# Dilated sliding attention into a two-layer feed-forward: new loads, transposes, masks and order for the first batches, and joined attention bursts

## Chip, core and metric

One core of one Trainium2 chip. The time is device microseconds (us) of the whole program. Before the change it is 368.92 us, the median of 3 runs (368.79 to 369.2).

## What is computed

```python
# q, k, v: (8 batches, 8 heads, 576 positions, 64), float32
scores = q @ k.T / sqrt(64)
rel = pos[:, None] - pos[None, :]
mask_plain = (rel >= 0) & (rel < 32)                      # heads 0-3
mask_dil = (rel >= 0) & (rel < 128) & (rel % 4 == 0)      # heads 4-7
attn = softmax(where(mask, scores, -1e9)) @ v
x = attn.transpose(0, 2, 1, 3).reshape(4608, 512)
h = x @ w_in                                               # (512, 2048)
out = maximum(0.01 * h, h) @ w_out                         # (2048, 512)
```

## The kernel before

Everything is float16 on TensorE (PE) with float32 sums. The attention is cut into 64 units. A number `n` = 2 * batch + kind names half a batch: four heads with the plain mask (kind 0) or with the dilated one (kind 1). A unit `u` is one pair of heads (`p`) and one half of the positions (288 of 576) of an `n`; there are 4 units in an `n` and 8 in a batch.

For each `n`, `load` fetches q, k and v on SP's queue, `cast_qk` and `cast_v` make them float16, and q and k are transposed so that the 64 head dimensions lie on partitions: for `n` < 4 (`NPE`) by PE (`pe_transpose`: six 96x96 blocks for two heads, then one copy from PSUM that spreads each block over every sixth column), later by a DMA transpose. `scores(u)` makes the 288 score columns of two heads in `sps` (six matmuls of 96 columns, or eight of 72 for kind 1), ACT takes the exponential (`er`), DVE multiplies by a 0/1 mask (`em`). `values(u)` makes the weighted values `o` and the sums `den`, takes the reciprocal (by ln and exp on ACT for batch 0, by DVE's reciprocal later) and DVE writes the product into `xT`. `sps`, `o` and `den` have one buffer each.

The feed-forward works on 9 chunks of 512 tokens. A chunk is 32 pieces of four matmuls with 512 columns: 16 of `ff_in` (one of 16 blocks of hidden units; ACT applies the leaky ReLU into `gt`), then 16 of `ff_out` (four groups of 128 tokens, each in four parts; ACT copies the sum to `ob`, and SP stores it). Chunk 0 needs all units of batch 0; chunk 1 needs batch 1 as well.

The order is written out by hand; each engine runs its instructions in this order, and SP issues its DMAs in it. Before the loop come the loads of batch 0, of w_in and w_out (1 MiB pieces through two staging buffers `wf`, so a third piece waits for the cast of the first) and of batch 1 (`load(2)`, `load(3)`), and the 8 units of batch 0. In the loop over chunks, chunk 0 has the work on batch 1 put between its pieces, two pieces to a unit of its second half; from chunk 1 on there are four pieces to a unit:

```python
if i % per == 0:
    if u + 1 < NU:
        scores(u + 1)
    prefetch(u // 4, u % 4)
if i % per == per // 2:
    values(u, False)
    u += 1
f()
```

So `scores` of the next unit and `values` of this one stand two pieces (8 matmuls) apart. After unit 63, in chunk 7, only feed-forward pieces are left.

Of the kernel before, what the change touches and what calls it, by code (L numbers as in the profile page):

```python
# [14 lines left out]
WIN = 32  # L15
# [6 lines left out]
CH = 512  # L22


@with_exitstack
def kernel(ctx: ExitStack, tc: tile.TileContext, q, k, v, w_in, w_out, out):
# [10 lines left out]
    ctx.enter_context(tc.manual_schedule())  # L37

    nc.scalar.preload_act_table_set("natural_log_exp_and_others")
    ones = cst.tile([128, 64], FP16, name="ones")  # L40
    nc.gpsimd.memset(ones, 1.0)

    mask = cst.tile([128, 3, 96], FP16, name="mask")
    nc.gpsimd.memset(mask, 1.0)
    nc.gpsimd.affine_select(out=mask, in_=mask, pattern=[[0, 3], [1, 96]], base=32,
                            channel_multiplier=-1, compare_op=ALU.is_ge, fill=0.0)
    nc.gpsimd.affine_select(out=mask, in_=mask, pattern=[[0, 3], [-1, 96]], base=-1,
                            channel_multiplier=1, compare_op=ALU.is_ge, fill=0.0)
    nc.gpsimd.memset(mask[0:32, 0, :], 0.0)
    ident = cst.tile([96, 96], FP16, name="ident")  # L50
    nc.gpsimd.memset(ident, 0.0)
    nc.gpsimd.affine_select(out=ident, in_=ident, pattern=[[-1, 96]], base=0,
                            channel_multiplier=1, compare_op=ALU.not_equal, fill=1.0)
# [3 lines left out]
    NPE = 4  # L57
# [12 lines left out]
    def load(n):  # L70
        b, kind = divmod(n, 2)
        base = (b * H + 4 * kind) * S * D
        for nm, x in (("q", q), ("k", k)):
            t = stg.tile([96, 24, D], FP32, tag=nm + "f")
            if n < NPE:
                nc.sync.dma_start(t.rearrange("p (h t) d -> p h (t d)", h=4),  # L76
                                  rows_ap(x, base, [[6 * D, 96], [S * D, 4], [1, 6 * D]]))
            else:
                nc.sync.dma_start(t, rows_ap(x, base, [[D, 96], [96 * D, 24], [1, D]]))
            qkf[n, nm] = t  # L80
        t = stg.tile([128, 32, D], FP32, tag="vf")
        vf[n] = t
        if kind == 0:
            s = base - 32 * D
            if s >= 0:
                nc.sync.dma_start(t[:, 0:24, :], rows_ap(v, s, [[D, 128], [96 * D, 24], [1, D]]))
            else:
                nc.gpsimd.memset(t[0:32, 0, :], 0.0)
                nc.sync.dma_start(t[32:128, 0, :], rows_ap(v, 0, [[D, 96], [1, D]]))
                nc.sync.dma_start(t[:, 1:24, :],  # L90
                                  rows_ap(v, s + 96 * D, [[D, 128], [96 * D, 23], [1, D]]))
        else:
            t4 = t.rearrange("p (g r) d -> p g (r d)", r=4)
            s = base - 128 * D
            if n < 2 * B - 1:
                nc.sync.dma_start(t4, rows_ap(v, s, [[4 * D, 128], [288 * D, 8], [1, 4 * D]]))
            else:
                nc.gpsimd.memset(t[96:128, 28:32, :], 0.0)
                nc.sync.dma_start(t4[:, 0:7, :],
                                  rows_ap(v, s, [[4 * D, 128], [288 * D, 7], [1, 4 * D]]))  # L100
# [4 lines left out]
    def cast_qk(n, *engs):  # L105
        for nm, eng in zip(("q", "k"), engs):
            t = att.tile([96, 2, 6, 2, D], FP16, tag=nm + "h", bufs=1)
            f = qkf.pop((n, nm))
            for p in range(2):
                src = f[:, 12 * p:12 * p + 12, :].rearrange("p (h t) d -> p h t d", h=2)  # L110
                dst = t[:, p].rearrange("p t h d -> p h t d")
                eng(out=dst, in_=src)  # L112
            qkh[n, nm] = t

    def cast_v(n, eng):
        t = att.tile([128, 32, D], FP16, tag="vh", bufs=3)
        m = 32 if n % 2 else 24
        eng(out=t[:, 0:m, :], in_=vf.pop(n)[:, 0:m, :])  # L118
        vh[n] = t

    def transpose(n):
        for nm, dst in (("q", qT), ("k", kT)):
            o = dst[n % NB][:, PAD:PAD + 2 * S].rearrange("p (c r) -> p c r", r=96)
            nc.sync.dma_start_transpose(
                o, qkh.pop((n, nm)).rearrange("p a t h d -> p (a t h d)"))

    def pe_transpose(n, p, nm, eng):

        h = qkh[n, nm]
        o = (qT if nm == "q" else kT)[n % NB][:, PAD + S * p:PAD + S * p + S]  # L130
        tp = psm.tile([128, 1024], FP16, tag="pm", name="tp")
# [7 lines left out]
    ems = {}  # L139

    def scores(u):
        n, p, half = u // 4, (u // 2) % 2, u % 2
        kind = n % 2
        sps = psa.tile([128, 2, 512], FP32, tag="sps")
        tok = PAD + S * p + HALF * half
        for j in range(4 if kind else 3):
            w = 72 if kind else 96
            for hh in range(2):
# [7 lines left out]
                nc.tensor.matmul(sps[:, hh, w * j:w * j + w], ka, qa, start=True, stop=True)  # L156
        er = att.tile([128, 2, HALF], FP16, tag="er", bufs=3)
        nc.scalar.activation(out=er, in_=sps[:, :, 0:HALF], func=AF.Exp, scale=SCALE)  # L158
        em = att.tile([128, 2, HALF], FP16, tag="em", bufs=3)
# [13 lines left out]
    def values(u, log_recip):  # L173
# [4 lines left out]
        o = psa.tile([128, 512], FP32, tag="o")  # L178
        den = psa.tile([128, 512], FP32, tag="den")
# [6 lines left out]
        for hh in range(2):  # L186
            nc.tensor.matmul(den[64 * hh:64 * hh + 64, 0:HALF], ones, em[:, hh, :],  # L187
                             start=True, stop=True)
        rec = att.tile([128, HALF], FP32, tag="rec")
        if log_recip:  # L190
            ln = att.tile([128, HALF], FP32, tag="ln")
# [17 lines left out]
    def load_w(i, g):  # L209
        t = stg.tile([128, 4, 512], FP32, tag="wf", bufs=2)  # L210
        if i == 0:
            src = rows_ap(w_in, 512 * g, [[DFF, 128], [128 * DFF, 4], [1, 512]])
        else:
            src = rows_ap(w_out, 512 * g * DM, [[DM, 128], [128 * DM, 4], [1, DM]])
        nc.sync.dma_start(t, src)
        wst[i, g] = t

    def cast_w(i, g, eng):
        eng(out=(w1, w2)[i][g], in_=wst.pop((i, g)))  # L219

# [3 lines left out]
    def ff_in(c, j):  # L224
# [3 lines left out]
        for i in range(4):  # L228
            nc.tensor.matmul(hp, w1[j // 4][:, i, 128 * (j % 4):128 * (j % 4) + 128],  # L229
# [5 lines left out]
    def ff_out(c, t, part):  # L235
# [6 lines left out]
        if part == 3:  # L242
            ob = moe.tile([128, DM], FP32, tag="ob", bufs=3, name="ob")
# [12 lines left out]
    V, P, A = nc.vector.tensor_copy, nc.gpsimd.tensor_copy, nc.scalar.copy  # L256
    load(0)
    load(1)
    for g in range(4):
        load_w(0, g)  # L260
    cast_qk(0, V, A)
    cast_v(0, P)
    for p in range(2):
        pe_transpose(0, p, "q", V)
        pe_transpose(0, p, "k", A)
    cast_qk(1, P, P)
    cast_v(1, P)
    scores(0)
    scores(1)
    for u in range(8):  # L270
        if u == 2:
            for p in range(2):
                pe_transpose(1, p, "k", A)
                pe_transpose(1, p, "q", V)
        if u + 2 < 8:
            scores(u + 2)
        values(u, True)
        if u == 3:
            cast_w(0, 0, P)
# [90 lines left out]
```

## Time and profile before

| | |
|---|---|
| median of 3 runs | 368.92 us |
| profiled execution: time / span | 367.16 / 365.5 us |
| PE busy / DVE / ACT / POOL | 320.9 / 213.5 / 160.0 / 86.1 us |
| feed-forward matmuls (L229, L240) | 1152 of 128x512, 385 ns each as recorded |
| units of attention | 64, of which 8 before chunk 0 |
| bytes read from HBM / written | 41.91 / 9.44 MB |

The span runs from the first instruction to the last; the rest of the profiled execution's time, 1.66 us, lies around it. Matmuls overlap in the pipeline, so their cost is read from the distance of their starts, not from the recorded duration. The profile's name `t` is that of any staging or float16 tile of q, k, v and the weights.

### The profile page before, as it was taken

How to read it: one execution, taken by the hardware profiler on the slowest of the kernel's cores; microseconds unless marked ns; L12 is line 12 of the kernel's file. 1: busy time of each engine (PE TensorE's matmuls, PEld its weight loads, DVE VectorE, ACT ScalarE, POOL GpSimd, SP SyncE). 2: the span in 40 equal slices, each digit the busy share in tenths (PEclk: the TensorE clock that was granted, in tenths of full speed). 3: DMA queues.
4: the chain of work that ended last, by engine and by line, in shares of the span. 5: the costliest groups of instructions: out<-in, count | busy, mean ns of one | idle time of the engine just before them, and what ended most of it. 6: DMA issues, size and time to landing. Idle time of an engine off the chain costs nothing.

```text
span 365.5 us, 5534 instructions
## 1 busy us (share of the span) xinstructions
PE 320.9 (88%) x2272; PEld 141.3 (39%) x2272; DVE 213.5 (58%) x204; ACT 160.0 (44%) x267; POOL 86.1 (24%) x97
## 2 busy tenths in 40 slices
PE   0453938857799999999999999999999999999995
PEld 0342314423344444444444444444444444444442
DVE  2575319999867777677667768766776674000000
ACT  1884623103365247425632562276236523713621
POOL 3442225545325031505220523045000000000000
PEclk9999987889999999999999999999999999999999
DMA  8984899999999289939972998495140011011011
GB/s 192 269 318 153 296 286 247 294 227 277 239 236 241 73 163 217 223 105 231 259 187 79 211 218 199 118 224 119 43 138 0 2 59 58 0 51 66 0 42 76
DMA packets 129727, 58.79 MB, mean 161 GB/s; under 512 B 109757, under 2 KB 120997, under 8 KB 129701
## 3 DMA queue, kind: packets, MB, share of 16 engines
q1 hardware_dynamic: 129701, 58.43, 63.9%
q8 instruction: 18, 0.29, 0.3%
q14 instruction: 8, 0.07, 0.1%
HBM read 41.91 MB, written 9.44 MB: 141 GB/s over the span
## 4 chain that ended last, share of the span: by engine, by line
PE 72%; DVE 11%; DMA 5%; ACT 5%; SPq 3%; issue 2%; POOL 0%; POOLq 0%; ACTq 0%
PE hp L229 31%; PE op L240 31%; DVE rec L195 5%; PE o L184 4%; PE sps L156 4%; DMA t<-in_k_dram 4%; SPq L76 3%; DVE xT L199 2%; PE den L187 2%; ACT kT L135 2%; DMA t<-in_moe_w_out_dram 1%; DVE qT L135 1%; ACT rec L193 1%; ACT ln L192 1%; DVE xT L202 1%
## 5 line engine op out<-in xcount | busy, mean ns | idle before, releaser
L229 PE MATMUL hp<-xT,w 128*128 128x512 f16 x576 | 137.0, 385 | 1.5 <-DVE xT L199 1.3
L240 PE MATMUL op<-w,gt 128*128 128x512 f16 x576 | 137.9, 385 | 0.0
L195 DVE RECIPROCAL rec<-den 128x288 f32<-128x288 f32 x56 | 109.5, 1955 | 42.0 <-PE den L187 42.0
L231 ACT ACTIVATE gt<-hp 128x512 f16<-128x512 f32 x144 | 86.0, 597 | 58.5 <-PE hp L229 57.7
L112 POOL CAST t<-t 96x768 f16<-96x768 f32 x58 | 48.8, 876 | 137.8 <-DMA qT<-t 122.7
L229 PEld LDWEIGHTS <-w 128*128 128x128 f16 x576 | 52.6, 99 | 65.1 <-issue 5.3
L240 PEld LDWEIGHTS <-gt 128*128 128x128 f16 x576 | 51.6, 98 | 62.2 <-issue 2.3
L244 ACT COPY ob<-op 128x512 f32<-128x512 f32 x36 | 21.1, 585 | 110.9 <-PE op L240 95.0
L158 ACT ACTIVATE er<-sps 128x576 f16<-128x576 f32 x64 | 42.0, 656 | 18.3 <-PE sps L156 18.3
L165 DVE TENSOR_TENSOR em<-er,mask 128x576 f16<-128x576 f16 x48 | 27.1, 564 | 13.7 <-ACT er L158 13.3
L184 PE MATMUL o<-em,t 128*64 128x72 f16 (+1 forms) x448 | 21.6, 216 | 14.7 <-DVE xT L199 7.8
L156 PE MATMUL sps<-qT,kT 64*128 64x72 f16 (+1 forms) x448 | 24.4, 231 | 6.3 <-ACT er L158 3.4
L118 POOL CAST t<-t 128x1536 f16<-128x1536 f32 (+1 forms) x16 | 27.0, 1688 | 9.2 <-DMA t<-in_v_dram 9.2
L184 PEld LDWEIGHTS <-t 128*64 128x64 f16 x448 | 13.9, 115 | 39.3 <-issue 13.3
L199 DVE TENSOR_TENSOR xT<-o,rec 128x288 f16<-128x288 f32 x32 | 25.7, 802 | 5.8 <-ACT rec L193 4.8
L156 PEld LDWEIGHTS <-kT 64*128 64x128 f16 x448 | 13.7, 109 | 31.1 <-issue 27.4
L133 PE MATMUL tp<-ident,t 96*128 96x96 f16 x96 | 8.5, 256 | 18.1 <-DVE t L112 14.2
L187 PE MATMUL den<-em,ones 128*64 128x288 f16 x128 | 20.3, 308 | 0.0
L135 DVE COPY qT<-tp 128x576 f16<-128x576 f16 x8 | 16.6, 2116 | 1.8 <-PE tp L133 1.8
L202 DVE TENSOR_TENSOR xT<-o,rec 128x288 f16<-128x288 f32 x32 | 14.6, 458 | 3.7 <-ACT rec L193 2.6
L133 PEld LDWEIGHTS <-t 96*128 96x128 f16 x96 | 7.0, 126 | 22.0 <-DVE t L112 14.6
L219 POOL CAST w<-t 128x2048 f16<-128x2048 f32 x4 | 7.6, 1893 | 21.7 <-DMA t<-in_moe_w_out_dram 15.9
(25 smaller groups left out, 54.0 us busy)
## 6 DMA issues: line engine op xcount, KB each, us to landing
t<-in_q_dram SPq DMA_DIRECT2D x16, 576.0 KB, 5.3
t<-in_k_dram SPq DMA_DIRECT2D x16, 576.0 KB, 7.1
out_dram<-ob SPq DMA_DIRECT2D x36, 256.0 KB, 2.0
t<-in_v_dram SPq DMA_DIRECT2D x7, 1024.0 KB, 9.0
t<-in_v_dram SPq DMA_DIRECT2D x7, 768.0 KB, 7.4
t<-in_moe_w_in_dram SPq DMA_DIRECT2D x4, 1024.0 KB, 11.3
t<-in_moe_w_out_dram SPq DMA_DIRECT2D x4, 1024.0 KB, 7.0
t<-in_v_dram SPq DMA_DIRECT2D x1, 896.0 KB, 8.3
```

Source lines behind the costliest of these rows:

```text
L112: eng(out=dst, in_=src)
L135: eng(out=o.rearrange("p (r t) -> p t r", t=6), in_=tp[:, 0:S].rearrange("p (t r) -> p t r", t=6))
L156: nc.tensor.matmul(sps[:, hh, w * j:w * j + w], ka, qa, start=True, stop=True)
L158: nc.scalar.activation(out=er, in_=sps[:, :, 0:HALF], func=AF.Exp, scale=SCALE)
L165: nc.vector.tensor_tensor(out=em.rearrange("p h (t c) -> p (h t) c", c=w), in0=er.rearrange("p h (t c) -> p (h t) c", c=w), in1=mb, op=ALU ...
L184: nc.tensor.matmul(o[64 * hh:64 * hh + 64, w * j:w * j + w], vt[:, sl, :], em[:, hh, w * j:w * j + w], start=True, stop=True)
L187: nc.tensor.matmul(den[64 * hh:64 * hh + 64, 0:HALF], ones, em[:, hh, :], start=True, stop=True)
L195: nc.vector.reciprocal(out=rec, in_=den[:, 0:HALF])
L199: nc.vector.tensor_tensor(out=x, in0=o[:, 0:HALF].rearrange("p (r u) -> p r u", r=4), in1=rec.rearrange("p (r u) -> p r u", r=4), op=ALU.mult)
L229: nc.tensor.matmul(hp, w1[j // 4][:, i, 128 * (j % 4):128 * (j % 4) + 128], xT[:, i, CH * c:CH * c + CH], start=(i == 0), stop=(i == 3))
L231: nc.scalar.activation(out=gts[c][:, j, :], in_=hp, func=AF.Prelu, alpha=0.01)
L240: nc.tensor.matmul(op, gts[c][:, j, 128 * t:128 * t + 128], w2[j // 4][:, j % 4, :], start=(j == 0), stop=(j == 15))
```

## The change

- For `n` < 5 q and k are loaded with nine rows (2304 B) to each of 128 partitions, where it was six rows (1536 B) on 96; batch 0 comes in four parts, one pair of heads each, q, k, v together. The PE transposes become 18 of 64x64 for a pair, and the copy from PSUM reads every 64th element and writes contiguously.
- Batch 0: a matmul of the identity with a bias tile (0 or -30000) opens each `sps`, the scores add to it, and the multiplication by the mask on DVE is gone. `o` and `den` come from the pool of four PSUM buffers. Reciprocals of units 1 and 4 are on DVE. More constants are built on POOL.
- 16 matmuls on a tile of zeros open the program.
- `wf` has three buffers; batch 1 is queued ahead of w_out; w_out is read in runs of 8 KiB to a partition. w_in's columns are taken with step 4 to fit.
- Chunk 0 is written out: 16 `ff_in`, units 8 and 9 bare, then `ff_out` in the order of the parts of w_out with four sums open, a unit to every two pieces. Batch 2's first half is transposed by PE in chunk 1, which has three pieces to a unit.
- From then on, `scores(u + 1)`, `values(u)` and the mask of `u + 1` (`masked`) follow on each other, four pieces apart; `den` comes before `o`. `ob` has two buffers instead of three.

```diff
-    NPE = 4
+    NPE = 5
...
+            elif len(pairs) == 2:
+                nc.sync.dma_start(t[:, 0:18, :].rearrange("p (a t) d -> p a (t d)", a=2),
+                                  rows_ap(x, base, [[9 * D, 128], [2 * S * D, 2], [1, 9 * D]]))
...
-        for t in range(6):
-            nc.tensor.transpose(tp[:, 96 * t:96 * t + 96],
-                                h[:, p, t].rearrange("p h d -> p (h d)"), ident)
-        eng(out=o.rearrange("p (r t) -> p t r", t=6),
-            in_=tp[:, 0:S].rearrange("p (t r) -> p t r", t=6))
+        for t in range(9):
+            for hh in range(2):
+                r = slice(64 * hh, 64 * hh + 64)
+                nc.tensor.transpose(tp[r, 64 * t:64 * t + 64], h[r, t, :], ident[r, r])
+        eng(out=o.rearrange("p (r t) -> p r t", t=9),
+            in_=tp[:, 0:S].rearrange("p (t r) -> p r t", t=9))
...
+        if pe_mask:
+            mb = ((bias0, bias), (bias40, bias4))[kind][half].rearrange("p a c -> p (a c)")
+            for hh in range(2):
+                nc.tensor.matmul(sps[:, hh, 0:HALF], ident, mb, start=True, stop=False)
...
-        t = stg.tile([128, 4, 512], FP32, tag="wf", bufs=2)
+        t = stg.tile([128, 4, 512], FP32, tag="wf", bufs=WF, name="wf")
...
-            nc.tensor.matmul(hp, w1[j // 4][:, i, 128 * (j % 4):128 * (j % 4) + 128],
+            nc.tensor.matmul(hp, w1[j // 4][:, i, j % 4::4],
...
+    castA(0)
+    transB(0)
+    castA(1)
+    C(0)
+    C(1)
+    transB(1)
+    Dv(0)
+    castA(2)
+    C(2)
+    Dv(1)
...
+    cast_w(0, 1, P)
+    load_qk(2)
+    load_v(2)
+    load_qk(3)
+    load_v(3)
+    cast_w(0, 2, V)
+    cast_w(0, 3, P)
+    for g in range(4):
+        load_w(1, g)
...
+    for g in range(4):
+        for t in range(4):
+            if t % 2 == 0 and u < 16:
+                if u + 1 < 16:
+                    scores(u + 1)
+                values(u, True)
+                if u + 1 < 16:
+                    masked(u + 1)
+                u += 1
...
+    for c in range(1, 9):
+        per, first = (3, 4) if c == 1 else (4, 0)
...
+            if u < NU and i >= first and (i - first) % per == 0 and not (c == 1 and i == 4):
+                if u + 1 < NU:
+                    scores(u + 1)
+                values(u, c == 1 and u % 2 == 0)
+                if u + 1 < NU:
+                    masked(u + 1)
+                prefetch(u // 4, u % 4)
+                u += 1
```

In the changed program `castA(x)` casts a pair of heads, `transB(x)` transposes it, `C(u)` is `scores` with the bias matmul and `Dv(u)` is `values` from the larger pool.

The order on SP's queue around the weights, before (L215 is `load_w`, the 96x4x384 loads are q and k of batch 1):

```order
L215 DMA t<-in_moe_w_in_dram 128x4x512 x4
L215 DMA t<-in_moe_w_out_dram 128x4x512 x4
L76 DMA t<-in_q_dram 96x4x384
L76 DMA t<-in_k_dram 96x4x384
L86 DMA t<-in_v_dram 128x24x64
```

The same place after:

```order
L255 DMA wf<-in_moe_w_in_dram 128x4x512 x4
L94 DMA qf<-in_q_dram 128x2x576
L94 DMA kf<-in_k_dram 128x2x576
L115 DMA vf<-in_v_dram 128x24x64
L94 DMA qf<-in_q_dram 128x2x576
L94 DMA kf<-in_k_dram 128x2x576
L126 DMA vf<-in_v_dram 128x8x256
L257 DMA wf<-in_moe_w_out_dram 128x2048 x4
```

Batch 1 moved from behind the four pieces of w_out to ahead of them.

PE in the loop around a burst of scores, before (`hp` and `op` are the sums of `ff_in` and `ff_out`):

```order
L229 MATMUL hp<-xT,w_0_101 128x512
L156 LDWEIGHTS kT_92
L156 MATMUL sps<-qT_89,kT_92 128x96
...
L229 LDWEIGHTS w_1_102
L229 MATMUL hp<-xT,w_1_102 128x512
```

and after:

```order
L189 LDWEIGHTS kT_117
L189 MATMUL sps<-qT_114,kT_117 128x96
L224 LDWEIGHTS ones
L224 MATMUL den<-em,ones 64x288
...
L230 LDWEIGHTS vh
L230 MATMUL o<-em,vh 64x72
L285 LDWEIGHTS gt
L285 MATMUL op<-w_0_129,gt 128x512
```

The scores are now followed by the sums and values of the unit before, and only then by feed-forward matmuls.

DVE in batch 0, before (L170 and L165 are the mask, L202 is xT, L135 the copy from PSUM):

```order
L112 CAST t<-t 96x2x6x64 x2
L135 COPY qT_89<-tp 128x6x96 x2
L170 TENSOR_TENSOR em<-er,mask 128x576
L165 TENSOR_TENSOR em<-er,mask 128x576
L170 TENSOR_TENSOR em<-er,mask 128x576
L202 TENSOR_TENSOR xT<-o,rec 128x288
```

and after:

```order
L136 CAST qh<-qf 128x576
L164 COPY qT_113<-tp 128x576
L136 CAST qh<-qf 128x576
L164 COPY qT_113<-tp 128x576
L164 COPY kT_116<-tp 128x576
L245 TENSOR_TENSOR xT<-o,rec 128x288
L136 CAST qh<-qf 128x576
L238 RECIPROCAL rec<-den 128x288
```

The masks are gone from DVE; casts of single pairs, more of the copies and two reciprocals stand there instead.

## Rows read from the trace of the kernel before

**Rows 1.** The page, part 2: 40 equal slices of the span (9.14 us each).

```profile
PE   0453938857799999999999999999999999999995
GB/s 192 269 318 153 296 286 247 294 227 277 239 236 241 73 163 217 223 105 231 259 187 79 211 218 199 118 224 119 43 138 0 2 59 58 0 51 66 0 42 76
```

**Rows 2.** Busy time of engines by stage; behind them granted clock, DMA share, GB/s.

```profile
0.00:38.20 38.20, 14.43 (x180) 9.83 (x181) 20.01 (x24) 21.85 (x31) 13.80 (x26) 1.00 0.80 240
38.20:96.70 58.50, 42.79 (x313) 18.53 (x312) 43.34 (x37) 16.77 (x29) 22.44 (x20) 0.88 1.06 264
96.70:361.50 264.80, 263.67 (x1786) 112.91 (x1780) 150.13 (x145) 120.75 (x207) 49.88 (x51) 1.00 0.54 128
361.50:365.50 4.00, 0.00 (x0) 0.00 (x0) 0.00 (x0) 0.58 (x1) 0.00 (x0) 1.00 0.17 68
```

**Rows 3.** Timeline of chunk 0's first half, engine by engine (start, duration, instruction).

```profile
32.21 13.86 SPq L215 DMA_DIRECT2D t<-in_moe_w_out_dram  x4
46.11 0.50 SPq L76 DMA_DIRECT2D t<-in_q_dram  x1
...
55.00 1.02 DVE L112 CAST t<-t 96x768 f16<-96x768 f32 x2 [1.08 <-DMA t<-in_q_dram]
...
55.61 0.66 PE L133 MATMUL tp<-ident,t 96*128 96x96 f16 x6 [7.14 <-DVE t L112]
...
66.99 1.89 POOL L118 CAST t<-t 128x2048 f16<-128x2048 f32 x1 [0.57 <-DMA t<-in_v_dram]
```

**Rows 4.** Groups of instructions by form: count, busy us, mean ns, idle before.

```profile
L195 DVE RECIPROCAL rec<-den 128x288 f32<-128x288 f32 x56 | 109.5, 1955 | 42.0 <-PE den L187 42.0
L158 ACT ACTIVATE er<-sps 128x576 f16<-128x576 f32 x64 | 42.0, 656 | 18.3 <-PE sps L156 18.3
L199 DVE TENSOR_TENSOR xT<-o,rec 128x288 f16<-128x288 f32 x32 | 25.7, 802 | 5.8 <-ACT rec L193 4.8
L135 DVE COPY qT<-tp 128x576 f16<-128x576 f16 x8 | 16.6, 2116 | 1.8 <-PE tp L133 1.8
L202 DVE TENSOR_TENSOR xT<-o,rec 128x288 f16<-128x288 f32 x32 | 14.6, 458 | 3.7 <-ACT rec L193 2.6
L135 ACT COPY kT<-tp 128x576 f16<-128x576 f16 x4 | 8.0, 2189 | 0.0
L112 DVE CAST t<-t 96x768 f16<-96x768 f32 x4 | 2.0, 552 | 7.5 <-DMA t<-in_q_dram 7.5
L112 ACT CAST t<-t 96x768 f16<-96x768 f32 x2 | 1.6, 828 | 6.9 <-DMA t<-in_k_dram 6.9
```

**Rows 5.** Timeline of ACT, end of batch 0.

```profile
33.93 0.41 ACT L192 ACTIVATE ln<-den 128x288 f32<-128x288 f32 x1 [1.61 <-PE den L187]
34.38 0.44 ACT L193 ACTIVATE rec<-ln 128x288 f32<-128x288 f32 x1
36.43 0.41 ACT L192 ACTIVATE ln<-den 128x288 f32<-128x288 f32 x1 [1.61 <-PE den L187]
```

**Rows 6.** Timeline of PE in the loop: eight matmuls and the scores after them.

```profile
134.97 1.90 PE L229 MATMUL hp<-xT,w 128*128 128x512 f16 x8
136.81 0.30 PE L156 MATMUL sps<-qT,kT 64*128 64x96 f16 x6
```

**Rows 7.** Timeline of ACT, end of chunk 8: two copies, 16 matmuls apart.

```profile
358.07 0.58 ACT L244 COPY ob<-op 128x512 f32<-128x512 f32 x1 [2.87 <-PE op L240]
361.52 0.58 ACT L244 COPY ob<-op 128x512 f32<-128x512 f32 x1 [2.87 <-PE op L240]
```

**Rows 8.** Timeline of PE: six transposes and what follows.

```profile
59.76 0.42 PE L133 MATMUL tp<-ident,t 96*128 96x96 f16 x6
60.01 1.03 PE L229 MATMUL hp<-xT,w 128*128 128x512 f16 x4
```

**Rows 9.** Timeline of DVE in chunk 0 (first), and the mask's line from 110 to 300 us.

```profile
87.36 1.70 DVE L165 TENSOR_TENSOR em<-er,mask 128x576 f16<-128x576 f16 x1
...
L165 DVE TENSOR_TENSOR em<-er,mask x34: 457/459/1731, 111.7 to 299.0; 128x576 f16<-128x576 f16 x34
```

More of the change, by code (lines that the diff above doesn't have):

```diff
@@ L177, in values @@
         vt = vh[n]
[L178 to L179 removed]
+        if pool is None:
+            o = psa.tile([128, 512], FP32, tag="o", name="o")
+            den = psa.tile([128, 512], FP32, tag="den", name="den")
+        else:
+            den = pool.tile([128, 512], FP32, tag="pm", name="den")
+            o = pool.tile([128, 512], FP32, tag="pm", name="o")
+        for hh in range(2):
+            nc.tensor.matmul(den[64 * hh:64 * hh + 64, 0:HALF], ones, em[:, hh, :],
+                             start=True, stop=True)
         for j in range(4 if kind else 3):
@@ L185, in values @@
                                  em[:, hh, w * j:w * j + w], start=True, stop=True)
[L186 to L189, printed above, removed]
+        rec = att.tile([128, HALF], FP32, tag="rec", name="rec")
         if log_recip:
-            ln = att.tile([128, HALF], FP32, tag="ln")
+            ln = att.tile([128, HALF], FP32, tag="ln", name="ln")
             nc.scalar.activation(out=ln, in_=den[:, 0:HALF], func=AF.Ln)
@@ new lines, with castA, transB, C @@
+    wp = psm.tile([128, 512], FP32, tag="pm", name="wp")
+    for _ in range(16):
+        nc.tensor.matmul(wp[0:64, 0:288], ones, warm, start=True, stop=True)
+    def castA(x):
+        n, p = divmod(x, 2)
+        cast_qk(n, "q", V, (p,))
+        cast_qk(n, "k", A, (p,))
+        cast_v(n, P, (p,))
+    def transB(x):
+        n, p = divmod(x, 2)
+        pe_transpose(n, p, "q", V)
+        pe_transpose(n, p, "k", V if x % 2 else A)
+    def C(u):
+        scores(u, True)
+    def Dv(u):
+        values(u, u not in (1, 4), psm)
@@ new lines @@
+    masked(8)
+    pe_transpose(3, 0, "q", V)
+    pe_transpose(3, 0, "k", A)
+    scores(9)
+    values(8, True)
+    masked(9)
+    pe_transpose(3, 1, "q", V)
+    pe_transpose(3, 1, "k", A)
+    scores(10)
+    values(9, True)
+    cast_v(3, P)
+    masked(10)
+    cast_w(1, 0, P)
+    load_qk(4)
+    load_v(4)
+    load_qk(5)
+    load_v(5)
+    u = 10
+    acc = [psm.tile([128, 512], FP32, tag="pm", name="op") for _ in range(4)]
+    for t in range(4):
+        ops[0, t] = acc[t]
+    for g in range(4):
+        for t in range(4):
+            if t % 2 == 0 and u < 16:
[5 more added lines that the diff above has]
+                u += 1
+            if t == 2 and g < 3:
+                cast_w(1, g + 1, P)
+            op = acc[t]
+            for j in range(4 * g, 4 * g + 4):
+                nc.tensor.matmul(op, gts[0][:, j, 128 * t:128 * t + 128], w2[g][:, j % 4, :],
+                                 start=(j == 0), stop=(j == 15))
+            if g == 3:
+                ob = moe.tile([128, DM], FP32, tag="ob", bufs=2, name="ob")
+                nc.scalar.copy(out=ob, in_=op)
+                nc.sync.dma_start(out[128 * t:128 * t + 128, :], ob)
```

292 lines of the change are left out of this document (154 added, 138 removed).

## The prediction

> **What bounds the kernel now.** I read the slices of the page first. PE's digits are 9 from about a quarter of the span to its end; before that they lie between 0 and 9 [rows 1]. The view by stages puts numbers to it: from 96.7 to 361.5 us PE is busy 263.67 of 264.8, in the 38.2 us of batch 0 only 14.43, and in chunk 0 (38.2 to 96.7) 42.79 of 58.5, at a mean granted clock of 0.88 against 1.00 afterwards; the last 4.0 us are a copy and a store [rows 2]. So the program is a start of 96.7 us in which PE waits, then a stretch in which PE is the bound.
>
> The start has two parts. In batch 0 nothing is saturated: DVE 20.01 and ACT 21.85 of 38.2 us [rows 2]. Its last units come every 2.5 us (ln at 33.93, the next at 36.43), and ACT waits 1.61 of these for the sums [rows 5]: a chain through one `o` and one `den`, not an engine. In chunk 0 PE stands 7.14 us until 55.61 for DVE's cast of batch 1, which itself waited for its load; that load was issued at 46.11, behind four pieces of w_out on SP from 32.21 on [rows 3]. Afterwards DVE is the bound: eight reciprocals of 1.955 us and eight copies from PSUM of 2.12 [rows 4] are 33 us of the stage's 43.34 [rows 2].
>
> In the long stretch a matmul costs 0.2156 us: 16 of them lie between two copies at the very end, 361.52 - 358.07 = 3.45 [rows 7]. Chunks 1 to 8 have 1024, or 220.8 us. The rest of 264.8 is 44.0 us for 48 units, 0.917 each.
>
> **Batch 0 (38.2 to about 26).** Work: DVE then has eight products (4 x 0.458 + 4 x 0.802), two reciprocals (3.91), four casts of 576 columns (0.75 x 0.552 = 0.41 each) and six copies; ACT has eight exponentials of 0.656, six pairs of ln and exp (0.41 + 0.44), four casts (0.62) and two copies [rows 4, 5]. The eight masks are gone; their replacement, two matmuls of 288 columns a unit, runs on a PE with 24 us free. POOL's longer list of constants and the 16 opening matmuls lie under the wait for the first load; each us they last beyond it delays batch 0 by one.
>
> The price of a copy is not in the trace. Above is 2.12 to 2.19, today's [rows 4]; below 0.66, the exponential that reads the same 576 columns from PSUM and writes them contiguously. I take 0.75, near the lower, since what slows today's looks like its scattered write: L199 and L202 read the same 288 columns and differ in the write alone, 0.802 against 0.458 [rows 4], and the new copy writes contiguously.
>
> The Trainium skill has a rule on this (SBUF — State Buffer, Door 1: The DMA port swizzle): SBUF is read in lines of 16 bytes and wants two hits in each, PSUM in lines of 8. The trace goes beyond it on the write side, since L199's step of 8 bytes puts two into a line and still costs 0.34 us more. On the read side the new step is 128 bytes, one element to a line, which the rule counts against the change; no row here shows such a read. With the rule the copies stay at 2.1 and the result is that of the first rival below.
>
> With 0.75, DVE has 15.1 us and ACT 14.5. Work can start when the first pair's q and k are in: half of today's transfer, so about 4.5 us, where DVE's first cast waits 6.4 now (7.5 idle before L112 for q [rows 4], less the 1.08 of chunk 0 [rows 3]). 4.5 + 15.1 = 19.6 is the lower end. The upper is today's pace: first exponential at about 8.7 (both casts, transposes and copies after 4.5), then eight units at 2.5 = 28.7. With two units in flight in four PSUM buffers it should be between; laying the chain out unit by unit (scores 0.5, exponential 0.66, ln and exp 0.85, product, each behind the casts and copies of its engine) I come to 26. The loads are no bound at 240 GB/s, today's mean with its gaps [rows 2]: 4.2 MB take 17.5 us, and the last pair's scores come near 21.
>
> **Chunk 0 (58.5 to about 45).** PE work: 128 x 0.2156 = 27.6; eight units of 0.80 (next part) = 6.4; eight groups of transposes. Six transposes cost 0.25 today, 59.76 to 60.01 [rows 8], 42 ns each; 18 of them are 0.75 a group if the smaller ones cost as much each (upper end; the lower is 0.25), 6.0 together. Sum 40.0. To this come waits: units 8 and 9 stand bare between transposes, where PE waits for exponential, mask, ln, exp and product in turn; two such chains of about 3 us, less the transposes beside them, and the start at the low clock, 5 us. So chunk 1 starts near 26 + 45 = 71, where it starts at 96.7 now. DVE, the bound today, drops out: the reciprocals move to ACT (0.85 instead of 1.955 on DVE), two of its eight copies go to ACT and all should shorten.
>
> Cover that this needs: loads. Today all of batch 0, w_in, w_out and batch 1 (16.8 MB) are in at 66.99 [rows 3], with a dip to 153 GB/s between two slices near 300 [rows 1], some 4 us, which a third staging buffer removes: 62.7, plus a cast of 1.9 gives 64.6. PE wants the last piece of w_out at about 67. The first half of batch 1, now ahead of w_out, is wanted at 26 + 48 x 0.2156 = 36; 9.6 MB at chunk 0's mean of 264 GB/s [rows 2], from about 2 us on, land at 38. So it fits to within 2 us, and it is the cover I trust least.
>
> **Chunks 1 to 8.** Eight matmuls between bursts take 136.81 - 134.97 = 1.84 [rows 6], where eight at the end take 1.725: 0.115 is lost at each interruption. A unit interrupts twice now and once after, so it should cost 0.917 - 0.115 = 0.80; 48 x 0.115 = 5.5 us gained. Bounds: 0, if going straight from scores to sums costs as much as both edges it replaces, and 11 us, if the attention bursts save the same again. Batch 2's first half adds four groups of transposes, 3.0, and three pieces to a unit in chunk 1 leave DVE's chain little room: 1.0. The stepped columns of w_in cost nothing while loading them hides behind the matmul before; what it lasts beyond 0.2156 would count 576 times. One `ob` less is hidden by the 4.25 us between copies; only at chunk 0's end, with copies four matmuls apart, does a third wait for the first store, at most the 4.0 us of copy and store at the end [rows 2]; I count it in the 5 us of waits.
>
> **Sum.** 71 + 220.8 + 48 x 0.80 (38.5) + 3.0 + 1.0 + 4.0 for the end = 338.3 us of span, against 365.5: 27.2 less. The profiled execution of 367.16 becomes 340.0; the median of before lies 1.76 above it, so 368.92 - 27.2 = 341.7.
>
> **Rivals.**
> - Copies stay slow, because any step costs, read or write. For: no row shows a stepped read that is fast. Against: L199 and L202. Price: 1.4 us a copy, four of them on batch 0's chain (5.6), two in the bare units (2.8), about 1.5 in chunk 1: 10 us, 351.5.
> - The loads pace the start, as they do at 55 us today. If they ran at 240 GB/s throughout, 16.8 MB would be in at 72 and cast at 74 where PE wants it at 67: 7 us, 348.7. Against: that mean holds a gap that goes.
> - The joined burst is paced by DVE. The mask of the next unit now comes last in its turn: sums 0.7 us after the turn begins, reciprocal 1.96, product 0.80, mask 0.46 make about 4.0 us, and PE wants it at 4.25 + 0.35 = 4.6. Masks of 1.70 do occur [rows 9]; if each were that long, the chain is 5.2, PE stands 0.6 a unit, and 48 units give back 28 us: from there on the change is slower than before, at 369.7 or more. Against: median 459 ns, 1.73 at worst of 34 [rows 9], and POOL, whose casts stand beside the long ones, is busy in a fifth of the stretch [rows 2].
> - The joining saves nothing and the rest comes as forecast: 347.
>
> **How the numbers follow.** Forecast 0.59 (own range 334 to 348), slow copies 0.15, loads 0.13, nothing from joining 0.09, DVE-paced loop 0.04. The range of 332 to 355 holds the first four but for their tails: batch 0 at 20 and cheap transposes would give 332, copies and loads both slow 359. A change under 0.2% (0.7 us) could not be told from none; it needs a loss that cancels 27 us almost exactly, 0.01. Slower is the DVE-paced loop and whatever like it I do not see, 0.04. Faster 0.95.
>
> **What would show it.** Right: chunk 1's first matmul near 71; copies from PSUM below 1 us; PE without an idle of 7 us in chunk 0 and SP issuing batch 1 before 30; 16 matmuls and a unit in about 4.25 in the loop; the same 4 us at the end. Wrong: copies of 2 us; PE idle before the first transposes of batch 1 or before a piece of w_out with a DMA as releaser; PE waiting for `em` in the loop; a granted clock below 1.00 through chunk 0.

## Result and profile after

The changed kernel takes 350.3 us (median of four runs, 349.54 to 352.44) against 368.86 of before beside it: 0.951 of the time, 95% interval 0.946 to 0.956. The gain is 18.6 us where the forecast had 27.2. The profiled execution took 349.84 us with a span of 348.1. In the table of the experiments the highest times of e1 and e2 are slow executions, over 1.5% above the fastest of the same kernel, which the ratios leave out and the medians do not.

The page's slices answer to [rows 1] (one slice is 8.7 us; PEclk is TensorE's granted clock in tenths):

```profile
PE   6789969999994699999999999999999999999995
...
PEclk9556998999998599999999999999999999999999
...
GB/s 218 363 365 315 392 351 242 176 186 179 173 245 211 171 260 182 167 206 248 207 100 196 232 197 137 202 211 0 118 73 2 2 76 44 2 60 60 2 60 61
```

After a start that is far shorter than before PE's digits drop twice: to 6 in the sixth slice (43.5 to 52.2 us, the bare units of chunk 0), and to 4 and 6 in the thirteenth and fourteenth, at 104 to 122 us, where the granted clock falls as well. The second hole was not there before. The windows view, with the stages of [rows 2] and that hole apart (columns as there):

```profile
0.00:29.20 29.20, 22.29 (x307) 13.93 (x308) 16.46 (x24) 14.50 (x27) 15.30 (x33) 0.65 0.99 325
29.20:72.00 42.80, 39.54 (x398) 19.80 (x398) 17.91 (x29) 22.95 (x44) 23.11 (x19) 0.92 1.01 277
72.00:108.10 36.10, 35.24 (x331) 17.65 (x329) 18.50 (x24) 19.13 (x36) 10.07 (x10) 1.00 1.09 200
108.10:120.00 11.90, 4.12 (x34) 1.98 (x34) 1.76 (x5) 3.58 (x7) 4.66 (x5) 0.62 0.92 190
120.00:344.10 224.10, 224.03 (x1502) 110.80 (x1500) 115.10 (x117) 103.02 (x177) 35.39 (x35) 1.00 0.62 121
344.10:348.10 4.00, 0.00 (x0) 0.00 (x0) 0.00 (x0) 0.59 (x1) 0.00 (x0) 0.80 0.18 68
```

Batch 0 ends at 29.2 (38.2 before), chunk 0 takes 42.8 (58.5), and all that follows 276.1, where 365.5 - 96.7 = 268.8 were needed before. So 9.0 + 15.7 us were won at the start and 7.3 given back behind it.

PE, ACT and SP around the hole (start, duration, instruction, idle time before it and what ended that):

```profile
105.67 2.54 PE L285 MATMUL op<-w,gt 128*128 128x512 f16 x11
115.92 0.42 PE L189 MATMUL sps<-qT,kT 64*128 64x96 f16 x6 [7.71 <-ACT er L192]
```

```profile
96.20 0.59 ACT L289 COPY ob<-op 128x512 f32<-128x512 f32 x1
...
100.51 0.58 ACT L289 COPY ob<-op 128x512 f32<-128x512 f32 x1 [1.56 <-PE op L285]
...
114.73 0.58 ACT L289 COPY ob<-op 128x512 f32<-128x512 f32 x1 [11.55 <-DMA out_dram<-ob]
115.21 0.66 ACT L192 ACTIVATE er<-sps 128x576 f16<-128x576 f32 x1
```

```profile
92.10 0.77 SPq L92 DMA_DIRECT2D qf<-in_q_dram  x1
92.92 1.83 SPq L92 DMA_DIRECT2D kf<-in_k_dram  x1
94.80 2.96 SPq L126 DMA_DIRECT2D vf<-in_v_dram  x1
97.80 1.47 SPq L92 DMA_DIRECT2D qf<-in_q_dram  x1
99.31 5.67 SPq L92 DMA_DIRECT2D kf<-in_k_dram  x1
105.08 2.92 SPq L115 DMA_DIRECT2D vf<-in_v_dram  x1
108.13 7.54 SPq L290 DMA_DIRECT2D out_dram<-ob  x3
```

Read from PE back: it waits for an exponential (`er`); that stands on ACT behind the third copy into `ob`; the copy waits for the first of the two `ob` to be stored; and the store, ready at 96.8, is issued at 108.13, since SP takes its list in order and six loads, of n = 7 and n = 8, stand ahead; at 96.8 SP is at the third of them. The store lands 6.5 us after its issue. The row of PE names ACT, the row of ACT names the store, and only SP's list shows the cause.

The groups that answer to [rows 4]:

```profile
L164 DVE COPY qT<-tp 128x576 f16<-128x576 f16 x10 | 7.5, 754 | 19.1 <-PE tp L162 19.1
L164 ACT COPY kT<-tp 128x576 f16<-128x576 f16 x4 | 2.5, 634 | 2.5 <-PE tp L162 2.4
```

The copies from PSUM take 0.75 us on DVE, 0.63 on ACT, a third of before.

### The profile page after: what moved, and what is told of

Read it like the earlier page. It is cut to its first block, busy times and chain, and to the rows that moved or that the text cites. A ratio compares the mean times of both kernels' runs of the same rounds, so it can differ in the third digit from the quotient of the medians.

```text
span 348.1 us, 6207 instructions
## 1 busy us (share of the span) xinstructions
PE 325.2 (93%) x2568; PEld 164.2 (47%) x2568; DVE 169.7 (49%) x196; ACT 163.8 (47%) x291; POOL 88.5 (25%) x101
## 4 chain that ended last, share of the span: by engine, by line
PE 78%; DMA 9%; ACT 4%; DVE 3%; SPq 3%; issue 1%; POOL 1%; ACTq 0%; POOLq 0%
PE hp L274 34%; PE op L285 29%; DMA vf<-in_v_dram 5%; PE sps L189 4%; PE den L224 4%; PE op L412 3%; DMA out_dram<-ob 2%; PE o L230 2%; PE tp L162 2%; DMA kf<-in_k_dram 1%; ACT rec L236 1%; ACT ln L235 1%; DVE xT L242 1%; POOL vh L148 1%; ACT er L192 1%
## 5 line engine op out<-in xcount | busy, mean ns | idle before, releaser
L238 DVE RECIPROCAL rec<-den 128x288 f32<-128x288 f32 x45 | 88.1, 1957 | 52.4 <-PE den L224 52.4
L274 PEld LDWEIGHTS <-w 128*128 128x128 f16 x576 | 63.3, 115 | 57.7 <-issue 4.3
L139 POOL CAST qh<-qf 96x768 f16<-96x768 f32 x22 | 18.4, 863 | 76.9 <-DMA qf<-in_q_dram 76.9
L148 POOL CAST vh<-vf 128x1536 f16<-128x1536 f32 (+3 forms) x18 | 27.4, 1521 | 36.7 <-DMA vf<-in_v_dram 19.1
L139 POOL CAST kh<-kf 96x768 f16<-96x768 f32 x22 | 18.1, 849 | 17.5 <-DMA kf<-in_k_dram 13.9
L204 DVE TENSOR_TENSOR em<-er,mask 128x576 f16<-128x576 f16 x42 | 21.0, 500 | 0.0
L230 PEld LDWEIGHTS <-vh 128*64 128x64 f16 x448 | 19.7, 119 | 1.1
L230 PE MATMUL o<-em,vh 128*64 128x96 f16 (+1 forms) x392 | 17.0, 204 | 0.0
L164 DVE COPY qT<-tp 128x576 f16<-128x576 f16 x10 | 7.5, 754 | 19.1 <-PE tp L162 19.1
L262 POOL CAST w<-wf 128x2048 f16<-128x2048 f32 x7 | 13.6, 1941 | 8.9 <-DMA wf<-in_moe_w_in_dram 6.0
```

Source lines behind the costliest of these rows:

```text
L139: eng(out=t[0:96, 12 * D * p:12 * D * p + 12 * D].rearrange("p (t h d) -> p h t d", t=6, h=2), in_=f[0:96, 12 * p:12 * p + 12, :].rearrang ...
L148: eng(out=vh[n][:, s, :], in_=vf[n][:, s, :])
L230: nc.tensor.matmul(o[64 * hh:64 * hh + 64, w * j:w * j + w], vt[:, sl, :], em[:, hh, w * j:w * j + w], start=True, stop=True)
L238: nc.vector.reciprocal(out=rec, in_=den[:, 0:HALF])
L274: nc.tensor.matmul(hp, w1[j // 4][:, i, j % 4::4], xT[:, i, CH * c:CH * c + CH], start=(i == 0), stop=(i == 3))
```

## The experiments

Each ran beside the kernel before on one chip (e1 to e4, e5 to e8, e9 to e12 on one each), so across these groups the ratios are compared; intervals are at 95%.

| run | edit | median (lowest to highest), us | ratio to before, interval |
|---|---|---|---|
| after | | 350.3 (349.5 to 352.4) | 0.951, 0.946 to 0.956 |
| e1 | three `ob` | 344.6 (344.0 to 350.2) | 0.933, 0.929 to 0.937 |
| e2 | one load later | 345.7 (343.2 to 352.6) | 0.934, 0.928 to 0.940 |
| e3 | e2, bursts apart | 350.4 (347.8 to 352.6) | 0.951, 0.945 to 0.957 |
| e4 | e2, contiguous reads | 345.4 (344.2 to 346.5) | 0.935, 0.931 to 0.939 |
| e5 | stores from ACT's queue | 340.5 (340.2 to 341.6) | 0.924, 0.919 to 0.929 |
| e6 | e1 and e2 | 342.6 (341.5 to 346.0) | 0.931, 0.924 to 0.938 |
| e7 | e1, w_out ahead | 350.2 (348.2 to 352.2) | 0.950, 0.943 to 0.958 |
| e8 | batch 0 masked by DVE, three `ob` | 347.3 (345.8 to 348.3) | 0.942, 0.936 to 0.948 |
| e9 | e5, no opening matmuls | 342.5 (341.5 to 343.4) | 0.930, 0.927 to 0.934 |
| e10 | e5, two `wf` | 341.1 (339.8 to 343.9) | 0.928, 0.924 to 0.932 |
| e11 | e5, units 8 to 10 masked by PE | 337.6 (335.6 to 340.2) | 0.917, 0.913 to 0.921 |
| e12 | e11, unit 0 first | 336.6 (335.9 to 338.3) | 0.914, 0.911 to 0.917 |

**The hole: e1, e2, e5, e6.** Theory: the store waits in SP's list. Three ways to remove that: a third buffer, fewer loads ahead, another queue.

```diff
-            ob = moe.tile([128, DM], FP32, tag="ob", bufs=2, name="ob")
+            ob = moe.tile([128, DM], FP32, tag="ob", bufs=3, name="ob")
```

(e1; `em` has two buffers and `ln` one, to make room.)

> The changed kernel with three buffers for ob instead of two (paid for with one buffer less of em and of ln, which have one reader each in their own order). Theory: the 7.7 us in which PE stands at 108 us come from ACT, whose third copy to ob waits for the first store of chunk 1, and SP issues that store only after the loads of two later half batches (the store at 108.1, the copy at 114.7). With a third buffer the third copy passes and the fourth waits for the same store: the stand shrinks by about one distance of copies, 3.5 to 4 us, so 346 us. Rival A: PE waits for q and k of the next half batch, whose transposes SP issues late; then nothing changes, 350. Rival B: the stand is the store's own time on a busy DMA; then a third buffer hides it all, 341.

```diff
-        if slot == 0 and n + 3 < 2 * B and n > 4:
+        if slot == 0 and n + 3 < 2 * B and n > 5:
...
-            if n == 4:
+            if n in (4, 5):
                 load_qk(n + 3)
                 load_v(n + 3)
```

(e2.)

> The changed kernel with two ob buffers, but the loads of half batch 8 are issued three units later, behind the transposes of half batch 7 and so behind three stores of chunk 1. Theory (stores behind two loads on SP): the first store goes out near 98 instead of 108, ACT does not wait, the 7.7 us of PE go, and with them some 2 us in which the eight bursts after the stand ran at the low granted clock: 9 to 10 us less than the changed kernel's 350.3, so 341. Rival A (late transposes): no change, 350. If the load of half batch 8 then comes too late for its own transposes, PE stands at the first unit of half batch 8 instead, and the gain is lost there.

```diff
-            nc.sync.dma_start(out[CH * c + 128 * t:CH * c + 128 * t + 128, :], ob)
+            nc.scalar.dma_start(out[CH * c + 128 * t:CH * c + 128 * t + 128, :], ob)
```

(e5, two `ob` as in the changed kernel.)

> The changed kernel with the stores of chunks 1 to 8 issued from ACT's queue, right behind the copy that fills `ob`, and still two `ob`. Theory (the stand of 7.7 us at 108 is the first store's wait behind loads in SP's queue): the store of the copy at 98 is issued at 99 and lands some 6.5 us later, as the one of 108.13 did, at 105; the third copy wants its buffer at about 107, so no stand, and the time is 350.3 - 7 = 343. Rival A (the transfer itself is late because the queues are full of loads): a stand of 2 to 4 us stays, 346 to 347. Rival B (ACT pays for the issue of each store ahead of the next exponential): no stand at 108, but PE waits for `er` at many places, 348 or more.

e6 has the edits of e1 and e2.

> Three `ob` (em in two, ln in one buffer) and the load of n=8 behind the transposes of n=7, so e1 and e2 together. Theory (each alone removed the stand of 7.7 us; the late load kept 3.6 of a later one, which the third buffer covers): no stand for `er` over 1 us anywhere, 343 to 344.5, that is e1's time or a little less. Rival (the two removals are separate gains): e1's 6 and e2's 5 add up, 340 or less.

All four lost the stand of 7.71. In e2 its place was taken by a smaller one a chunk later, from the timeline of PE:

```profile
148.91 0.30 PE L189 MATMUL sps<-qT,kT 64*128 64x96 f16 x6 [3.59 <-ACT er L192]
```

and there SP issued the store of the copy at 132.72 only at 141.55, behind a transpose and three loads. So moving one load only moved the place, and e2 missed the 341 expected; e6 with a third buffer has no such stand, as forecast, and its gains do not add up (342.6). e1 was 5.7 us faster than the changed kernel by medians (6.9 by ratio), not 4: no rest of the wait stayed, against my expectation of 3.5 to 4 us. Its first store of chunk 1 still leaves 7.0 us after its copy (106.27, behind a copy at 98.71 of 0.59 us), but nothing waits for it.

e5 tells most. ACT in that run:

```profile
95.94 0.58 ACT L289 COPY ob<-op 128x512 f32<-128x512 f32 x1
...
96.56 0.38 ACTq L290 DMA_DIRECT2D out_dram<-ob  x1
...
100.25 0.58 ACT L289 COPY ob<-op 128x512 f32<-128x512 f32 x1 [1.55 <-PE op L285]
100.86 0.34 ACTq L290 DMA_DIRECT2D out_dram<-ob  x1
...
105.02 0.58 ACT L289 COPY ob<-op 128x512 f32<-128x512 f32 x1 [1.94 <-PE op L285]
```

The store leaves 0.04 us after the copy, the third copy waits for PE and no longer for a store, and the issue costs ACT 0.34 us that nothing waits for. The loads on SP are the same six, there are still two `ob`, and the transfers are no shorter: the first three stores of chunk 1 land 4.3, 7.2 and 5.5 us after their issue. So the place in the queue is shown to make the store late, and e1 shows that the late store costs PE nothing with a third buffer; the hole needs both. 340.5 is below the 343 expected, because the hole had cost more than its 7.71 us: the low clock behind it some 2 us (from 115.92 to 124.06 the changed kernel needs 8.14 for what takes 5.7 at the later pace), and with the loads in other places the wait of 0.81 for a transpose by DMA, until 90.94, went too. e1, e6, e7 and e8, all with three `ob`, have two waits of 0.85 us for DVE's copies of batch 2 near 74 to 84 us that the others have not; why, I did not settle.

**The joined bursts: e3.** From chunk 2 on the sums and values stand two pieces behind the scores again, on top of e2:

```diff
                 if u + 1 < NU:
                     scores(u + 1)
-                values(u, c == 1 and u % 2 == 0)
+                if c == 1:
+                    values(u, u % 2 == 0)
...
+            if c > 1 and u < NU and i % 4 == 2:
+                values(u)
+                u += 1
```

> As e2_late_load, but from chunk 2 on values(u) stands two pieces (8 matmuls) behind scores(u+1) again, as before the change: 39 units interrupt the feed-forward twice. Theory: each interruption of the feed-forward costs 0.115 us, so 39 x 0.115 = 4.5 us more than e2_late_load (345.5 if that is 341), and eight matmuls between bursts take 1.84 us. Rival: going from scores straight to the sums costs as much as both edges; then the time is that of e2_late_load.

The medians differ by 4.7 us and the ratios by 0.017, or 6.3 us; the intervals do not overlap. The same unit of the loop, e2 first, then e3:

```profile
163.54 0.44 PE L189 MATMUL sps<-qT,kT 64*128 64x72 f16 x8
...
167.87 0.44 PE L189 MATMUL sps<-qT,kT 64*128 64x72 f16 x8
```

```profile
161.29 0.45 PE L189 MATMUL sps<-qT,kT 64*128 64x72 f16 x8
161.67 1.92 PE L274 MATMUL hp<-xT,w 128*128 128x512 f16 x8
163.52 0.31 PE L224 MATMUL den<-em,ones 128*64 128x288 f16 x2
...
165.74 0.44 PE L189 MATMUL sps<-qT,kT 64*128 64x72 f16 x8
```

4.33 against 4.45 us for the same work: 0.12 for one interruption less, 4.5 for 39 units at the 0.115 of the prediction. From these points to the end e3 has 27 interruptions more, 3.1 us at 0.115, and the two profiled executions take 181.7 and 184.7 us. What e3 may have lost beyond the 4.5 us is not explained.

**The step of the copies: e4.** The read from PSUM is contiguous here and nothing puts the positions back in order: in the five halves that PE transposes, q and k stand at other positions than v and the mask take them for.

```diff
-        eng(out=o.rearrange("p (r t) -> p r t", t=9),
-            in_=tp[:, 0:S].rearrange("p (t r) -> p r t", t=9))
+        eng(out=o, in_=tp[:, 0:S])
```

> As e2_late_load, but the copies from PSUM after PE's transposes read their 576 columns in order instead of with a step of 64 (leaves out: the reordering of the columns, so the positions come out permuted). Theory: the step on the read side costs nothing, only a scattered write does: the copies stay at 0.76 us on DVE and 0.64 on ACT, and the time is that of e2_late_load within 0.5 us. Rival (short lines of PSUM): the copies fall to below 0.6 us, and batch 0, with four copies on its chain, gets about 1 us shorter.

```profile
L164 DVE COPY qT<-tp 128x576 f16<-128x576 f16 x10 | 4.5, 453 | 16.7 <-PE tp L162 16.7
...
L164 ACT COPY kT<-tp 128x576 f16<-128x576 f16 x4 | 2.6, 639 | 2.3 <-PE tp L162 2.2
```

The stepped read costs DVE 0.30 us a copy, against my expectation of nothing, and ACT nothing. The time is the same all the same (345.4 and 345.7), and batch 0 ends at 28.86 (28.99 in e2), not the 1 us earlier of the rival: the 16 copies of DVE do not set the pace there.

**What the start needs: e7, e8, e10.** e7 is e1 with three pieces of w_out ahead of batch 1:

```diff
-    load_qk(2)
-    load_v(2)
-    load_qk(3)
-    load_v(3)
     cast_w(0, 2, V)
     cast_w(0, 3, P)
-    for g in range(4):
+    for g in range(3):
         load_w(1, g)
+    load_qk(2)
+    load_v(2)
+    load_qk(3)
+    load_v(3)
+    load_w(1, 3)
```

> e1 (three `ob`), and three of the four pieces of w_out queued on SP ahead of batch 1 as before the change; the fourth stays behind batch 1. Theory (batch 1 ahead of w_out matters): its first half, cast from 31.0 on now, comes three pieces of some 3.4 us later, at about 41 to 42, with the cast at 43; PE's first transposes of it are due at 40, so PE stands 3 us and the time is 344.6 + 3 = 347.6. Rival (the slack of some 9 us that q and k of batch 1 had covers it all but): within 1 us of e1, and then it is the shorter batch loads and the third buffer that removed the 7.14 us of before, not the order.

It loses 6.5 us by ratio (0.950 against 0.933). From its timeline of PE:

```profile
43.63 0.47 PE L162 MATMUL tp<-ident,kh 64*64 64x64 f16 x18 [2.48 <-POOL kh L136]
...
54.78 0.45 PE L224 MATMUL den<-em,ones 128*64 128x288 f16 x2 [2.79 <-DVE em L204]
58.68 0.45 PE L224 MATMUL den<-em,ones 128*64 128x288 f16 x2 [2.85 <-DVE em L209]
```

The first wait is the one expected; the rest is dearer than I thought. The second half's transposes and the bare units come late as well, and there two of DVE's masks take 1.91 and 2.00 us (at 52.82 and 56.63; 0.45 each in e1) while POOL casts v and w_out (52.53 to 60.39): PE's two waits for `em` are 1.28 and 1.53 us in e1.

e8 gives batch 0's masks to DVE again:

```diff
-        scores(u, True)
+        scores(u)
+        masked(u)
```

> Three `ob` (room for them from the bias tiles that go, em and ln as in the changed kernel), and batch 0's masks by DVE again, multiplied onto the exponentials, in place of the two matmuls of 288 columns a unit; POOL's five bias tiles go too. Theory (the mask by PE shortens batch 0): DVE gets eight products of about 0.46 us, 3.7 in all, each in the chain between exponential and sums; batch 0 ends 1.5 to 3 us later than e1's 27.9, and the time is 346 to 348. Rival (PE, at the lower granted clock in 10 to 30 us, pays as much for the 16 bias matmuls, 0.2 to 0.3 each, and POOL's bias tiles hold the first scores back by 0.5): batch 0 ends where e1's does or earlier, 343.5 to 345.

Its batch 0 ends at 32.46 us, against 27.92 in e1 and 29.20 in the changed kernel, and PE waits for `em` 1.41, 1.99 and 1.50 us in three of the last units; the time is within the 346 to 348 expected, though batch 0 ends 4.5 us later than in e1, not 1.5 to 3. By ratio the masks by PE are worth 3.3 us (0.0091 x 368), with intervals that just touch.

e10 has `WF = 2` in place of 3, on top of e5.

> e5 with two staging buffers for the weights in place of three, as before the change. Theory (the third buffer is needed: with two, each piece of w_in and w_out waits for the cast two pieces ahead, and all loads queued behind it on SP wait too): the loads of w_out and then of batch 2 come 3 to 5 us later, PE stands at the first piece of w_out or at batch 2, 343 to 346. Rival (slack covers it: q of batch 1 is cast 8 us before it is wanted, w_out 6 us): 340.5 within 0.7.

SP spends 15.47 us on w_in's four pieces (13.28 in e5), batch 1 leaves at 25.16 (23.00 in e5), and PE does not notice: chunk 1 starts at 71.96 (72.62 in e5). The intervals overlap; the slack covers the third buffer's share.

**The granted clock: e9.**

```diff
-    wp = psm.tile([128, 512], FP32, tag="pm", name="wp")
-    for _ in range(16):
-        nc.tensor.matmul(wp[0:64, 0:288], ones, warm, start=True, stop=True)
```

> e5 (stores from ACT's queue) without the 16 opening matmuls. Theory (they lie under the wait for the first load and buy nothing: the granted clock is 0.50 from 10 to 30 us in spite of them): the time is e5's 340.5 within 0.7. Rival (they help the first transposes and scores, whose granted clock was 0.96 in 0 to 10 us): batch 0 ends some 1 to 1.5 us later, 341.5 to 342.

Windows of e5, then of e9 (columns as above):

```profile
10.00:20.00 10.00, 9.34 (x164) 6.01 (x165) 6.51 (x9) 6.26 (x13) 2.91 (x3) 0.50 1.06 378
20.00:30.00 10.00, 8.30 (x95) 4.51 (x91) 7.74 (x9) 4.60 (x11) 5.17 (x3) 0.52 0.98 346
```

```profile
10.00:20.00 10.00, 8.29 (x176) 5.31 (x174) 6.79 (x10) 6.55 (x13) 3.29 (x4) 1.00 1.07 377
20.00:30.00 10.00, 7.71 (x75) 4.12 (x76) 8.02 (x9) 4.78 (x10) 5.30 (x3) 0.54 1.07 372
```

Without the opening matmuls the granted clock falls later, batch 0 ends 0.5 us earlier (28.71 against 29.20) and chunk 1 starts 1.3 earlier (71.33 against 72.62). So in these two executions they buy nothing there. Their effect on the clock is not shown. The granted clock of a view does not give PE's pace this early, as e9's timeline of PE has it:

```profile
10.76 0.69 PE L162 MATMUL tp<-ident,qh 64*64 64x64 f16 x18
11.26 0.67 PE L162 MATMUL tp<-ident,kh 64*64 64x64 f16 x18
...
14.76 0.47 PE L162 MATMUL tp<-ident,qh 64*64 64x64 f16 x18 [0.64 <-DVE qh L136]
15.07 0.45 PE L162 MATMUL tp<-ident,kh 64*64 64x64 f16 x18
```

At 10.76 the 18 transposes take 0.50 us from start to start beside a granted clock of 1.00, as much as the changed kernel's at 0.50 (10.81 to 11.31); four us later they take 0.31. And e12 below has the opening matmuls too and is granted 1.00 until 20 us. PE stood 2.24 us for `er` before 9.89 in the changed kernel, only 0.74 at that place in e12.

The ratio is higher all the same, 0.930 against 0.924 with intervals that overlap, and neither the theory's 340.5 nor the rival's later end of batch 0 came. The trace has a wait of 1.89 us for a transpose by DMA, until 91.35, that e5 has not: SP issues it at 86.06 (86.35 in e5), while PE wants it 1.3 us earlier. The 12 matmuls behind it take 4.38 us, against 2.69 in e5. These 3.6 us use up the 1.3 and make most of the 2.1 us by which this span is longer. Whether the other executions lose by the same wait stays open.

**A faster version: e11, e12.** e11 is e5 with `scores(u, True)` for units 8, 9 and 10 and without their `masked`; e12 moves one line as well.

```diff
-    scores(9)
+    scores(9, True)
     values(8, True)
-    masked(9)
```

> e5 with the masks of units 8, 9 and 10, which stand bare between transposes in chunk 0, added by PE as in batch 0, in place of DVE's product. Theory (DVE's mask is in the chain there: PE waited 0.97, 1.12 and 1.78 for `em` in e5, 3.9 in all): those waits shrink to what the exponential alone takes, PE pays six matmuls of 288 columns (some 0.15 each): 2 to 3 us less, 338. Rival (the exponential and the sums' buffers keep the chain as long): 340 to 340.5.

```diff
-    castA(1)
     C(0)
+    castA(1)
     C(1)
```

> e11, and in batch 0 the scores and exponential of unit 0 put ahead of the casts of the second pair, so that ACT's cast of k, which waits for its load until 8.6, no longer stands ahead of the first exponential. Theory (that wait is on batch 0's chain: PE waits 2.4 for `er` at 9.9): batch 0 ends 1 to 1.5 us earlier, about 27.5, and the time is 1 to 1.5 below e11's, some 337. Rival (the later casts and copies of DVE and ACT set batch 0's end anyway): e11's time within 0.5.

e11 is 2.9 us below e5 by medians, 2.6 by ratio, in the range expected, but the intervals still overlap a little. The profiled executions do not show the gain: e11's, at 340.23 the longest of its six, has e5's span of 338.5. There the bare stretch from the scores of unit 8 to `ff_out` does shrink, from 8.7 us (43.43 to 52.17) to 7.0 (44.86 to 51.88), and the three waits for `em`, 3.9 us together, leave one of 0.27 for `er` and one of 0.65 for the `o` buffer. But the 45 matmuls of `ff_in` ahead take 11.48 us against 10.09, at a granted clock that rises later, and new waits of 0.69 and 1.27 come at 54.84 and 61.35. In e12 batch 0 ends at 27.05, 2.3 earlier than in e11 (29.33), but the median gains only 1.0, at the edge of the 1 to 1.5 expected, and the intervals overlap. With 336.6 us, 0.914 of before, it has the lowest time of all.

## Why the prediction was right in kind and short in size

| stage | forecast | after | e5 |
|---|---|---|---|
| batch 0 ends | 26 | 29.2 | 29.2 |
| chunk 0 | 45 | 42.8 | 43.4 |
| chunks 1 to 8 and the end | 267.3 | 276.1 | 265.9 |
| span | 338.3 | 348.1 | 338.5 |

The 350.3 lies outside the forecast's own 334 to 348 and close to two rivals, 348.7 and 351.5, of which neither happened: the copies are fast and the loads early. That the range of 332 to 355 holds it is luck as to the mechanism, since none of its rivals is a late store.

- **The step that failed** is the one on `ob`: "One `ob` less is hidden by the 4.25 us between copies; only at chunk 0's end … does a third wait for the first store, at most the 4.0 us of copy and store at the end". I priced a store by its own length and took for granted that it is issued when its copy is done. In SP's list it stood 11.3 us behind loads. The trace of before could not show this. There SP was through its loads when the store came, which left 0.03 us after its copy (at 119.31, 0.58 us), and so did the first store of every later chunk:

```profile
112.16 3.27 SPq L86 DMA_DIRECT2D t<-in_v_dram  x1
119.92 9.16 SPq L245 DMA_DIRECT2D out_dram<-ob  x3
```

  The wait cost 7.71 us, and more at the granted clock of 0.62 behind it: 16 matmuls took 4.23 us until 124.06, and 3.58 in the loop (158.61 to 162.19). With the store on another queue the stage takes 265.9, 1.4 less than forecast. I looked for late loads and never asked what the loads make late once PE comes 24.7 us earlier to chunk 1. At chunk 0's end the step held: ACT waited 1.6 us for stores there, and PE not at all.
- **Batch 0** was 3.2 us short. I let the masks run "on a PE with 24 us free"; PE was then busy 22.29 of 29.2 us (4.05 of it the opening matmuls), at a mean granted clock of 0.65, and my chain priced its bursts near the pace of the loop. The 1.00 of [rows 2] does not stand for that pace. In batch 0 of the kernel before (first two rows) a burst of scores takes 0.35 us to the next start, in the changed kernel at a granted 0.50 (last two) 0.36, and in the loop 0.23 (136.81 to 137.04, [rows 6]):

```profile
16.23 0.42 PE L156 MATMUL sps<-qT,kT 64*128 64x96 f16 x6 [0.74 <-ACT er L158]
16.58 0.45 PE L184 MATMUL o<-em,t 128*64 128x96 f16 x6
...
13.13 0.42 PE L189 MATMUL sps<-qT,kT 64*128 64x96 f16 x6
13.49 0.45 PE L224 MATMUL den<-er,ones 128*64 128x288 f16 x2
```

  So the low pace is not the change's doing; the change gave PE more to do at it. From about 10 to 30 us a group of 18 transposes took 0.50 to 0.60 us from start to start, and at the high level 0.30 to 0.39. What the pace alone cost is not shown: e9 had the high one from 14.76 to about 20 us and ended batch 0 only 0.5 us earlier. More hung on one cast of ACT that waited for its load ahead of the first exponential. In e12, without it, PE's wait for `er` falls from 2.38 (e11) to 0.74 us and batch 0 ends 2.3 earlier; the granted clock from 10 to 20 us differs too, 0.50 and 1.00, so how much of the rest is the cast's stays open. I had not laid out the order of `castA(1)` and `C(0)` by engine. (ACT's work in the prediction adds up to 14.3, not 14.5; DVE's 15.1 is the longer either way.)
- **Chunk 0** was 2.2 us too long: eight transpose groups at 0.75 were 6.0; from the rows below two take 0.69, so 2.8 in all. This and the late batch 0 nearly cancel, by luck, so that chunk 1 starts at 72.0 for a forecast of 71.

```profile
40.61 0.47 PE L162 MATMUL tp<-ident,qh 64*64 64x64 f16 x18
40.91 0.45 PE L162 MATMUL tp<-ident,kh 64*64 64x64 f16 x18
41.30 1.05 PE L274 MATMUL hp<-xT,w 128*128 128x512 f16 x4
```

- **The copies** came at 0.754 us for a forecast of 0.75. The Trainium skill's rule (SBUF — State Buffer, Door 1: The DMA port swizzle), by which every access that crosses to a new line pays a penalty, gives no size for it. The 2.1 that the prediction put beside it did not come; measured, the stepped read costs 0.30 us on DVE and nothing on ACT (e4). The rest of the 2.12 of before went with the scattered write, as L199 and L202 said.
- **The loads**, the cover trusted least, held: DVE casts q of batch 1 at 31.0 and PE takes it at 40.6. e7 shows that this is the order's doing, e10 that the third `wf` is not needed for it. The loads ran at 325 and 277 GB/s in the first two stages, not at 240 to 264.
- **Joining** was right in size by the pitch of the loop (e3). The loop was not paced by DVE: PE is busy 224.03 of 224.1 us from 120 on.

## What to carry to other kernels

When a buffer is taken away, ask for the time from the copy's end to the landing of its store, and read it in the list of the queue that issues the store: what stands ahead of it there counts, not the transfer alone. Read it at the times after the change. In the kernel before, these stores left at once; with the shorter start and the new order of loads, which no run takes apart, the first came to stand behind loads. Here it paid to put the stores on a queue that carries no prefetch (e5). And when work moves to an engine that is "free", price it by that engine's own durations in that stretch.

## What was not expected of the hardware

- Copy of 128x576 f16 from PSUM: with elements 128 bytes apart 754 ns on DVE and 634 on ACT, contiguous 453 and 639.
- The granted clock of a view can stand at 1.00 early in a program while PE works at its low pace: 18 transposes took 0.50 us from start to start at 10.76 in e9, 0.31 at 14.76, both beside 1.00.
